# Low parts of v and of the softmax factors: identity products summed in PSUM in place of VectorE subtractions

## The chip, the cores and the metric

The kernel runs on one core of a Trainium2 chip. A core has five engines that run side by side, each through its own list of instructions: TensorE (PE, matrix products, results in PSUM), VectorE (DVE), ScalarE (ACT), GpSimd (POOL) and SyncE (SP, which here only starts transfers). They wait for each other by semaphores. The metric is the device time of one execution in microseconds; the lower the better.

## The reference

For each of 8 batches and 8 heads, with 576 positions, 64 values per head and 32 memory slots, all in fp32:

```python
a = softmax(phi)                                  # over the 32 slots
k_m = einsum('bhsm,bhsd->bhmd', a, k)
v_m = einsum('bhsm,bhsd->bhmd', a, v)
attn = softmax(q @ k_m.T / sqrt(64))
x = attn @ v_m                                    # heads side by side: (8, 576, 512)
scores = x @ w_gate
for b in range(8):                                # the 128 best positions of each batch
    h = relu(xe @ w1);  ye = h @ w2               # xe: the chosen rows; F = 1024
    out[b, top] = xe + sigmoid(score) * ye
```

The choice of the best 128 positions depends on small differences of the scores, so the kernel keeps close to fp32 all the way to the choice. That is why v and the softmax factors are split into two parts each before their product.

## The kernel before, in words

There are 16 groups, one for each batch and half of its heads (four heads). For each group the function `softmax` computes the softmax factors `e` in a [128, 576] tile (four heads x 32 slots by positions). It is long: 48 VectorE instructions per group with ScalarE instructions between them, since the exponential and its rounding are followed step by step. It ends with L276, and goes on to `keys`.

`keys` turns `e` on TensorE (L316, six 96-column blocks, two PSUM banks), copies it to SBUF with ScalarE (L318, tile `aS`), and then splits it: `hi` is `aS` with the lowest twelve mantissa bits cleared (L322, a bitwise and on VectorE), `lo` is `aS - hi` (L324, a subtraction on VectorE). GpSimd starts eight transfers that write `lo` and `hi` to the DRAM tensor `aparts` (L327). TensorE then multiplies `aS` with k (L333), and ScalarE stores the result in `kbd` (L338).

`split_v` does the same with v: a [128, 1152] tile per group is loaded (L285), `hi` by a bitwise and (L293), the low part by a subtraction in place (L295), and GpSimd starts the writes of both to `vparts` (L298). The next tile is loaded into one of two buffers.

`values` reads `vparts` and `aparts` back in another layout and sums the products of the parts over the positions (L371, 9216 small products in four stages of two batches). Attention (`centre`, `scores`, `attend`, `rank`, `gather`) and the expert layer (`ffn`, L625, L636, L646) follow for each batch.

The order of the work is written out by hand: every function is a generator, and a `yield` gives way. One pass of the main loop is called a turn here. In each turn, one call goes to the softmax (two chains of groups alternate at first: one has groups 0, 2, 4, 6 and then 8 to 15, the other 1, 3, 5, 7), one call in every second turn to `split_v`, then 7 calls (10 with attention, 12 once the softmax is done) to the sums, one to the attention and two to the expert layer. Attention starts when the short chain is done. The instructions enter each engine's list in this order, and a later instruction doesn't overtake an earlier one's place in its engine's list. A group takes 11 calls here, a v tile three.

The kernel has eight banks of PSUM: four hold the sums of `values`, and the other four go round as `bank` for all else until the sums are done.

Of the kernel before, what the change touches and what calls it, by code (L numbers as in the profile page):

```python
# [8 lines left out]
F32 = mybir.dt.float32  # L9
# [5 lines left out]
AF = mybir.ActivationFunctionType  # L15
# [4 lines left out]
P = 128  # L20
NC = 6
# [16 lines left out]
def kernel(  # L38
# [15 lines left out]
    nc = tc.nc  # L54
    ctx.enter_context(tc.manual_schedule())
    B, S, D = out.shape
# [6 lines left out]
    Dh = D // H  # L63
# [5 lines left out]
    scale = 1.0 / Dh ** 0.5  # L69
# [7 lines left out]
    const = ctx.enter_context(tc.tile_pool(name="const", bufs=1))  # L77
    weights = ctx.enter_context(tc.tile_pool(name="weights", bufs=1))
    rows = ctx.enter_context(tc.tile_pool(name="rows", bufs=1))
# [7 lines left out]
    vio = first.enter_context(tc.tile_pool(name="vio", bufs=2))  # L87
    more = []

    def bank(shape, dtype=F32, pool=None):  # L90
        pool = pool or (more or [pss])[0]
        return pool.tile(list(shape), dtype, tag="bank", name="bank")
# [11 lines left out]
    def load_q(b, j):  # L104
        qs[b, j] = step.tile([P, NPR, S // 2], F32, name="qb")
        nc.sync.dma_start(out=qs[b, j], in_=qT[b, :, :, j * (S // 2):(j + 1) * (S // 2)])

    groups = [(b, g) for b in range(B) for g in range(NG)]
# [4 lines left out]

    ident = const.tile([P, P], F32, name="ident")
    make_identity(nc, ident)

    kbd = [const.tile([P, NPR, 2 * M], F32, name=f"kbd{i}") for i in range(B)]
    vbd = [const.tile([P, 2, 4 * Dh], F32, name=f"vbd{i}") for i in range(3)]
# [63 lines left out]
    def softmax(i, ch):  # L182
# [3 lines left out]
        def t(name, dtype=F32):  # L186

            return ex.tile([P, NC * P if name in WIDE else S], dtype, name=name)[:, :S]
# [56 lines left out]
        dl, p = t("lo"), t("big")  # L245
# [29 lines left out]
            stt(out=e, in0=a0, scalar=sm[:, part:part + 1], in1=e, op0=ALU.mult, op1=ALU.add)  # L275
        stt(out=e, in0=e, scalar=sm[:, 1:2], in1=a0, op0=ALU.mult, op1=ALU.add)  # L276
        soft[i] = e
        yield
        yield from keys(i, ch)

    def split_v():

        def load(b, g):
            vb = vio.tile([P, 4 * S * Dh // P], F32, name="vb")
            nc.sync.dma_start(out=vb, in_=v[b, g])  # L285
            return vb

        coming = load(*groups[0])
        for i, (b, g) in enumerate(groups):
            vb = coming  # L290
            yield
            hi = vio.tile([P, 4 * S * Dh // P], F32, name="vhi")
            nc.vector.tensor_single_scalar(hi.bitcast(I32), vb.bitcast(I32), -4096,  # L293
                                           op=ALU.bitwise_and)
            nc.vector.tensor_sub(vb, vb, hi)  # L295
            yield
            for vp, src in enumerate((vb, hi)):
                nc.gpsimd.dma_start(  # L298
                    out=vparts[b, g, :, vp].rearrange("w r s d -> w (r s d)")
                                           .rearrange("w (p x) -> p w x", p=P),  # L300
                    in_=src.unsqueeze(1).to_broadcast([P, 2, 4 * S * Dh // P]))
            if i + 1 < len(groups):
                coming = load(*groups[i + 1])
            yield

    v_m = {}

    def keys(i, ch):
        ex, (b, g) = exs[ch], groups[i]
        a = soft.pop(i)  # L310
        kb = ks.pop(i)
        aS = ex.tile([P, NC * P], F32, name="lo")[:PT].rearrange("p (c m) -> p c m", m=P)
        for c0 in range(0, NC, 3):
            tp = bank([PT, 3, P])
            for c in range(3):
                nc.tensor.transpose(out=tp[:, c], in_=a[:, (c0 + c) * PT:(c0 + c + 1) * PT],  # L316
                                    identity=ident)
            nc.scalar.activation(aS[:, c0:c0 + 3], tp, AF.Copy)  # L318
        yield
        hi = ex.tile([P, NC * P], F32, name="big")[:PT].rearrange("p (c m) -> p c m", m=P)  # L320
        lo = ex.tile([P, NC * P], F32, name="low")[:PT].rearrange("p (c m) -> p c m", m=P)
        nc.vector.tensor_single_scalar(hi.bitcast(I32), aS.bitcast(I32), -4096,  # L322
                                       op=ALU.bitwise_and)
        nc.vector.tensor_sub(lo, aS, hi)  # L324
        for part, src in enumerate((lo, hi)):
            for h in range(4):
                nc.gpsimd.dma_start(  # L327
                    out=aparts[h, b, g, part].rearrange("(c p) m -> p c m", p=PT),
                    in_=src[:, :, h * M:(h + 1) * M])
        km = bank([P, 2, 2 * M])  # L330
        for rr in range(2):
            for c in range(NC):
                nc.tensor.matmul(out=km[:, rr], lhsT=kb[:, c, rr * P:(rr + 1) * P],  # L333
                                 rhs=aS[:, c, rr * 2 * M:(rr + 1) * 2 * M],
                                 start=(c == 0), stop=(c == NC - 1))
        for u in range(2):
            part = slice(u * Dh, (u + 1) * Dh)
            nc.scalar.activation(kbd[b][part, 2 * g:2 * g + 2, u * M:(u + 1) * M],  # L338
                                 km[part, :, u * M:(u + 1) * M], AF.Copy)
# [345 lines left out]
    def finish(job):  # L685
        for _ in job:
            pass
# [3 lines left out]
    def group(i, ch):  # L691
        at = order[ch].index(i)
        if at + 1 < len(order[ch]):
            load_phi(order[ch][at + 1], ch)
        yield from softmax(i, ch)
        made.append(i)

    def softmaxes():

        todo, live, since = [list(o) for o in order], {}, 6  # L700
        while any(todo) or live:
            for ch in range(2):
                if ch not in live and todo[ch] and since >= 6:
                    live[ch] = group(todo[ch].pop(0), ch)
                    since = 0
            since += 1
            for ch in list(live):
                if next(live[ch], live) is live:
                    del live[ch]
                yield  # L710

    def steps():

        return 12 if not working else 10 if attend_all else 7
# [13 lines left out]
    def attentions():  # L728

        todo, live, since = list(range(B)), [], 12  # L730
        while todo or live:
            if todo and todo[0] in summed and len(live) < 2 and since >= (12 if working else 8):
                live.append(attention(todo.pop(0)))
                since = 0
            since += 1
            for job in list(live):
                if next(job, live) is live:
                    live.remove(job)
            yield

    late_consts()
    w1_sb = weights.tile([P, KD, F], F32, name="w1_sb")
    w2_sb = weights.tile([P, KF, D], F32, name="w2_sb")
    working = [softmaxes(), split_v()]
    parts, sums, attend_all, products = None, all_sums(), None, ffns()
    turn = 0
    while True:
        turn += 1
        if turn == 8:
            nc.scalar.activation(ident16, ident, AF.Copy)  # L750
            nc.sync.dma_start(out=w1_sb, in_=w1.rearrange("(t p) f -> p t f", p=P))
            nc.sync.dma_start(out=w2_sb, in_=w2.rearrange("(t p) f -> p t f", p=P))
        if working and next(working[0], working) is working:
            working.pop(0)
        if len(working) == 2 and turn % 2:
            next(working[1], None)
        for _ in range(steps()):
            next(sums, None)
        if attend_all is None and set(order[1]) <= set(made):

            finish(working.pop(1))
            first.close()
            work, step, one = (
                ctx.enter_context(tc.tile_pool(name=name, bufs=2 - (name == "one"),
                                               reuse_waits="tile"))
                for name in ("step", "work", "one"))
            for j in range(2):
                load_q(0, j)
            eTs = [one.tile([P, 2, NT * P], F32, name=f"eT{i}") for i in range(2)]
            for t in eTs:  # L770
                nc.gpsimd.memset(t[:, :, S:], 0.0)
            attend_all = attentions()
        if attend_all and next(attend_all, working) is working:
            break
        for _ in range(2):
            next(products)
# [3 lines left out]
    ps = bank([1, B * NT])  # L780
# [46 lines left out]
```

## Time and profile before

The median of three runs is 1050.5 us (1049.24 to 1057.09). The profiled execution has a span of 1051.3 us.

| Engine | busy, us | share of the span |
|---|---|---|
| VectorE | 784.4 | 75% |
| TensorE products | 598.7 | 57% |
| TensorE weight loads (overlap the products) | 439.8 | 42% |
| ScalarE | 293.6 | 28% |
| GpSimd | 224.3 | 21% |

| Queue | MB | share of 16 DMA engines |
|---|---|---|
| started by SyncE | 94.14 | 29.5% |
| started by GpSimd | 70.27 | 19.7% |

A busy share is an average over the whole span. The rows of instructions give a line, the engine, what it writes and reads with its shape, how often, then the busy time and the mean of one in ns, then how long the engine was idle just before and what ended that. A row of waits gives who waited, for whom, the sum in us, how many times and the longest. An fp32 product shows as two records where the operands are plain fp32.

### The profile page before, as it was taken

Reading aid. Unit: us, or ns where it says so; the run is one execution under the profiler, and the core shown is the slowest. Engines: PE = TensorE matmul, PEld = TensorE weight load, DVE = VectorE, ACT = ScalarE, POOL = GpSimd, SP = SyncE. Lnnn points to the kernel's source line nnn. Section 1 sums busy time; section 2 is a strip of 40 time slices with the busy share of each in tenths; the row PEclk is TensorE's granted clock in tenths of the full one; section 3 lists DMA queues with packets and bytes.
Section 4 is the critical chain, followed back from the end, with each engine's and each line's share of the span. In section 5 each row is a group of like instructions: output and inputs, shape, how many; then the busy total and the mean of one; then the engine's idle time right before and its main releaser. Section 6 shows DMA issues by size and latency. Waiting matters only on the chain. (4 is left out here: it accounts for less than half of the span.)

```text
span 1051.3 us, 25384 instructions
## 1 busy us (share of the span) xinstructions
PE 598.7 (57%) x10738; PEld 439.8 (42%) x10738; DVE 784.4 (75%) x1342; ACT 293.6 (28%) x578; POOL 224.3 (21%) x335
## 2 busy tenths in 40 slices
PE   0021022255554355675567397875738969889795
PEld 0021022154443354554434374664415657544542
DVE  7899999899899968698786968698993336324940
ACT  2233233233233232323224342141432101213230
POOL 7030221220230230404113021402503011011110
PEclk9999999995665656877678699566866986989688
DMA  9364544677887825554613256463404466522320
GB/s 291 126 232 153 188 157 169 192 230 277 264 274 253 313 46 155 152 179 145 214 51 106 72 141 206 127 194 115 114 0 116 153 218 189 163 66 66 120 70 23
DMA packets 60714, 166.11 MB, mean 158 GB/s; under 512 B 10801, under 2 KB 21041, under 8 KB 60593
## 3 DMA queue, kind: packets, MB, share of 16 engines
q1 hardware_dynamic: 39088, 94.14, 29.5%
q0 software_dynamic: 21504, 70.27, 19.7%
q8 instruction: 87, 1.43, 0.6%
q14 instruction: 35, 0.28, 0.1%
HBM read 96.21 MB, written 68.16 MB: 156 GB/s over the span
## 5 line engine op out<-in xcount | busy, mean ns | idle before, releaser
L371 PE MATMUL acc<-a_rows,v_rows 32*64 32x128 f32 x9216 | 217.8, 257 | 106.7 <-DMA a_rows<-aparts 97.6
L371 PEld LDWEIGHTS acc<-a_rows,v_rows 32*64 32x64 f32 x9216 | 197.7, 167 | 150.2 <-issue 113.9
L316 PE MATMUL bank<-ident,e 128*96 128x128 f32 x96 | 22.5, 403 | 214.8 <-DVE e L276 204.6
L316 PEld LDWEIGHTS bank<-ident,e 128*96 128x96 f32 x96 | 16.0, 185 | 219.7 <-issue 183.4
L333 PE MATMUL bank<-lo,kb 96*128 96x64 f32 x384 | 67.0, 353 | 7.6 <-ACT lo L318 6.8
L333 PEld LDWEIGHTS bank<-lo,kb 96*128 96x128 f32 x384 | 65.5, 267 | 12.1 <-ACT lo L318 8.6
L327 POOL DMA_DIRECT2D aparts<-low x64 | 47.2, 746 | 104.5 <-DVE low L324 100.8
L646 PE MATMUL bank<-w_sb,hT 128*128 128x512 f32 x128 | 67.2, 661 | 0.0
L636 PE MATMUL bank<-w_sb,xeT 128*128 128x512 f32 x128 | 65.5, 647 | 2.9 <-ACT xeT L627 2.9
L530 PE MATMUL bank<-vbd,eT 128*128 128x256 f32 x160 | 60.0, 510 | 0.0
L221 DVE TENSOR_TENSOR lo<-lo,rh 128x576 f32<-128x576 f32 x64 | 56.7, 885 | 2.2
L176 ACT ACTIVATE vh<-num 128x576 int16<-128x576 f32 x32 | 21.8, 683 | 127.3 <-DVE num L225 116.7
L534 DVE TENSOR_TENSOR xj<-bank,rd 128x512 f32<-128x512 f32 x40 | 27.5, 688 | 36.8 <-PE bank L530 34.9
L537 POOL TENSOR_TENSOR xj<-xj,mean 128x1024 f32<-128x1024 f32 (+1 forms) x12 | 26.1, 2174 | 128.5 <-DVE xj L534 89.8
L583 DVE SCALAR_TENSOR_TENSOR cmp<-row,tg,wide 128x576 bf16<-128x576 f32 x40 | 32.5, 811 | 25.9 <-ACT row L569 25.1
L298 POOL DMA_DIRECT2D vparts<-vb x16 | 11.6, 726 | 186.2 <-DVE vb L295 161.9
L224 DVE TENSOR_TENSOR low<-low,lo 128x576 f32<-128x576 f32 x64 | 48.5, 758 | 2.2
L327 POOL DMA_DIRECT2D aparts<-big x64 | 46.7, 738 | 0.0
L220 DVE SCALAR_TENSOR_TENSOR lo<-num,vh 128x576 f32<-128x576 f32 x48 | 36.0, 751 | 13.2 <-ACT vh L176 13.2
L530 PEld LDWEIGHTS bank<-vbd,eT 128*128 128x128 f32 x160 | 35.0, 243 | 23.8 <-issue 19.6
L602 PE MATMUL bank<-tg,pick 128*128 128x2 f32 (+1 forms) x80 | 16.9, 329 | 47.4 <-DVE pick L597 20.2
L176 ACT ACTIVATE low<-big,c 128x576 f32<-128x576 f32 x16 | 12.4, 775 | 96.4 <-DVE big L247 96.4
(150 smaller groups left out, 1244.2 us busy)
## 6 DMA issues: line engine op xcount, KB each, us to landing
v_rows<-vparts SPq DMA_DIRECT2D x128, 288.0 KB
vparts<-vb POOLq DMA_DIRECT2D x16, 1152.0 KB, 5.2
vparts<-vhi POOLq DMA_DIRECT2D x16, 1152.0 KB, 8.9
a_rows<-aparts SPq DMA_DIRECT2D x512, 36.0 KB
vb<-in_v SPq DMA_DIRECT2D x16, 576.0 KB
kb<-in_k SPq DMA_DIRECT2D x16, 576.0 KB
qb<-in_qT SPq DMA_DIRECT2D x16, 576.0 KB
out<-xj POOLq DMA_DIRECT2D x16, 512.0 KB, 3.8
```

The costliest lines, as they stand in the source:

```text
L176: nc.scalar.activation(dst, src, func, bias=biases[c] if c else 0.0, scale=s)
L220: stt(out=lo, in0=val, scalar=GRID, in1=h, op0=ALU.mult, op1=ALU.subtract)
L221: tt(out=lo, in0=lo, in1=rh, op=ALU.mult)
L224: tt(out=low, in0=low, in1=lo, op=ALU.add)
L316: nc.tensor.transpose(out=tp[:, c], in_=a[:, (c0 + c) * PT:(c0 + c + 1) * PT], identity=ident)
L327: nc.gpsimd.dma_start(out=aparts[h, b, g, part].rearrange("(c p) m -> p c m", p=PT), in_=src[:, :, h * M:(h + 1) * M])
L333: nc.tensor.matmul(out=km[:, rr], lhsT=kb[:, c, rr * P:(rr + 1) * P], rhs=aS[:, c, rr * 2 * M:(rr + 1) * 2 * M], start=(c == 0), stop=(c = ...
L371: nc.tensor.matmul(out=accs[i][:Dh, :P].rearrange("p (h m) -> p h m", m=M), lhsT=vr[p, s], rhs=ar[p, :, s], start=(ch == 0 and s == 0), st ...
L530: nc.tensor.matmul(out=o[:, g * 4 * Dh:(g + 1) * 4 * Dh], lhsT=eT[:, g, (c0 + c) * P:(c0 + c + 1) * P], rhs=vbd[b % 3][:, g], start=False, ...
L583: nc.vector.scalar_tensor_tensor(out=cmp, in0=row, scalar=g, in1=wide[:, off:off + S], op0=ALU.is_equal, op1=ALU.mult, accum_out=equal[:, ...
L636: nc.tensor.matmul(out=ps[:n], lhsT=xeT[:, d, :n], rhs=w1_sb[:, d, f0:f0 + 512], start=(d == 0), stop=(d == KD - 1))
L646: nc.tensor.matmul(out=ps[:n], lhsT=hT[:, f, :n], rhs=w2_sb[:, f], start=(f == 0), stop=(f == KF - 1))
```

## The change

The subtractions leave VectorE. A new function `difference` makes x - y as two products that add up in one PSUM bank: the identity times x, and then the negated identity times y. ScalarE copies the bank to the place of the result, one `yield` later. The low part of v is made in three pieces of 384 columns, that of the softmax factors in two pieces of 384. The masks that make the high parts stay on VectorE. A constant `less_ident` is added. The `yield` after the end of the softmax goes away, and `split_v` is called in every turn, not in every second one. The purpose is to take work off VectorE and give it to TensorE and ScalarE.

```diff
     make_identity(nc, ident)
+    less_ident = const.tile([P, P], F32, name="less_ident")
+    nc.scalar.activation(less_ident, ident, AF.Copy, scale=-1.0)
...
         soft[i] = e
-        yield
         yield from keys(i, ch)
...
             vb = coming
             yield
-            hi = vio.tile([P, 4 * S * Dh // P], F32, name="vhi")
+            hi = vio.tile([P, n], F32, name="vhi")
             nc.vector.tensor_single_scalar(hi.bitcast(I32), vb.bitcast(I32), -4096,
                                            op=ALU.bitwise_and)
-            nc.vector.tensor_sub(vb, vb, hi)
-            yield
+            for x0 in range(0, n, n // 3):
+                x = slice(x0, x0 + n // 3)
+                yield from difference(vb[:, x], hi[:, x], vb[:, x])
             for vp, src in enumerate((vb, hi)):
                 nc.gpsimd.dma_start(
...
+    def difference(x, y, dst):
+
+        rows, n = x.shape
+        ps = bank([rows, n])
+        nc.tensor.matmul(out=ps, lhsT=ident[:rows, :rows], rhs=x, start=True, stop=False)
+        nc.tensor.matmul(out=ps, lhsT=less_ident[:rows, :rows], rhs=y, start=False, stop=True)
+        yield
+        nc.scalar.activation(dst, ps, AF.Copy)
...
         nc.vector.tensor_single_scalar(hi.bitcast(I32), aS.bitcast(I32), -4096,
                                        op=ALU.bitwise_and)
-        nc.vector.tensor_sub(lo, aS, hi)
+        for c0 in range(0, NC, 3):
+            yield from difference(*(x[:, c0:c0 + 3].rearrange("p c m -> p (c m)")
+                                    for x in (aS, hi, lo)))
         for part, src in enumerate((lo, hi)):
...
-        if len(working) == 2 and turn % 2:
+        if len(working) == 2:
             next(working[1], None)
```

More of the change, by code (lines that the diff above doesn't have):

```diff
@@ L286, in load @@
             return vb
-        coming = load(*groups[0])
+        coming, n = load(*groups[0]), 4 * S * Dh // P
         for i, (b, g) in enumerate(groups):
@@ L300, in split_v @@
                                            .rearrange("w (p x) -> p w x", p=P),
[L301 removed]
+                    in_=src.unsqueeze(1).to_broadcast([P, 2, n]))
             if i + 1 < len(groups):
```

## The prediction

> **What bounds the kernel now.** I read the totals and the slices first, then the same sums over three stretches, because the totals average over stages with different limits. The stretches are cut where the eighth and the sixteenth softmax group end (337.0 and 789.7 us are the starts of the instruction that ends them, L276; the last of their key products follows some 10 us later).
>
> ```profile
> PE 598.7 (57%) x10738; PEld 439.8 (42%) x10738; DVE 784.4 (75%) x1342; ACT 293.6 (28%) x578; POOL 224.3 (21%) x335
> ...
> PE   0021022255554355675567397875738969889795
> ...
> DVE  7899999899899968698786968698993336324940
> ```
>
> ```profile
> 15.00:345.00 330.00, 103.46 (x2362) 95.32 (x2363) 302.04 (x457) 100.02 (x160) 65.82 (x101) 0.87 0.64 218
> 345.00:802.00 457.00, 289.99 (x5530) 218.16 (x5529) 369.62 (x657) 140.26 (x291) 115.19 (x148) 0.72 0.45 135
> 802.00:1051.30 249.30, 205.24 (x2849) 126.30 (x2848) 101.71 (x226) 51.83 (x126) 28.93 (x52) 0.86 0.37 117
> ```
>
> The columns after the length are the busy times of PE, PE's weight loads, DVE, ACT and POOL, then granted clock, DMA share and GB/s. Stage one (two softmax chains and the splitting of v) is VectorE: 302 of 330 us, 92%. Stage two (one chain, with attention) is VectorE at 81% with PE at 63%. Stage three has no softmax; PE is busy 82% of it, VectorE 41%.
>
> The chain of work that ended last reaches back only to 939 us and is mostly the expert layer's products (L646, L636), so it says nothing about the changed lines. The waits say more:
>
> ```profile
> PE bank L316 <- DVE e L276: 204.6, 12, 58.4
> DVE rd L522 <- PE bank L517: 25.2, 8, 5.5
> DVE big L322 <- ACT lo L318: 6.0, 5, 2.2
> SPq L285 <- DMA vparts<-vb: 153.9, 8, 28.2
> ```
>
> PE waits for VectorE at 12 of 16 groups, so up to there PE is ahead. VectorE's waits for PE and ScalarE are short and lie in the attention; between 200 and 300 us, say, all its listed waits come to 5.6 us. The last line: the load of the next v tile starts when the write of an older one has landed.
>
> **What the Trainium skill says.** "VectorE: DVE Perf Modes", the section on the 1x mode, gives one fp32 result per cycle for an operation on two tensors, at 0.96 GHz: 1152 elements are 1.20 us, and the trace has 1.36 for the subtraction of v (L295). The one-tensor mask (L293) takes 0.77 for the same size. So the subtraction is the dear half of the split. "TensorE: Matmul & The Clock Gate", Part 1, says that PE runs at half rate after an idle window of about 3.4 us and at full rate after a busy one. The trace agrees in its durations: four records of one shape (L646) take 3.62 us at 756 us and 1.98 at 766 us; its clock column, which shows 1.00 for the nearly idle first 200 us, does not show this. The same page ("Architectural detail") calls ScalarE's and VectorE's queues strictly first in, first out. In the trace no ScalarE copy overtakes one that waits for PE (L338 waited 48.8 us in 14 times). That is the danger here: a copy out of PSUM that waits holds the softmax's own ScalarE work.
>
> **The change part by part.**
>
> ```profile
> L295 DVE TENSOR_TENSOR vb<-vb,vhi 128x1152 f32<-128x1152 f32 x16 | 21.7, 1358 | 0.6
> L324 DVE TENSOR_TENSOR low<-lo,big 96x768 f32<-96x768 f32 x16 | 15.3, 954 | 0.5
> L293 DVE TENSOR_SCALAR vhi<-vb 128x1152 int32<-128x1152 int32 x16 | 12.2, 765 | 0.0
> L318 ACT ACTIVATE lo<-bank 96x384 f32<-96x384 f32 x32 | 14.5, 484 | 25.7 <-PE bank L316 25.6
> ```
>
> Removed: 16 subtractions of 1.358 us for v (21.7 us, all before 348 us) and 16 of 0.954 us for the softmax factors (15.3 us, half in each of the first two stages). Stage one loses 21.7 + 7.6 = 29.3 us of VectorE, stage two 7.6.
>
> Added on PE: 48 pairs of products for v (three thirds of 16 tiles) and 32 for the factors, each 384 columns wide in fp32. A pair leaves four records, since one fp32 product leaves two (64 products with w2 are 128 records of L646). The row with four records of 512 columns, scaled by 384/512, gives 1.98 x 0.75 = 1.5 us with PE busy, and 3.62 x 0.75 = 2.7 after idling. 80 pairs are 120 to 216 us. In stage one 64 pairs at 2.7 are 173 us on top of 103, which fits into 300; in stage two 16 pairs at 1.5 are 24 us on top of 290 of 457. As an average it hides behind VectorE.
>
> Added on ScalarE: 80 copies from PSUM of the shape of L318, 0.484 us each: 39 us, 31 of them in stage one, which goes from 100 to 131 us of about 310. It hides too, unless a copy waits for PE. The one-time negated identity costs a ScalarE instruction of some 0.3 us (the cast of the identity, L750, takes 292 ns) before the first softmax needs that engine: nothing.
>
> Moved: the copy comes one turn after its pair, so PE has a turn's time. A softmax group takes 12 calls instead of 11: two yields more in the key part, one fewer after e. A v tile takes 5 turns instead of 6 (five calls at every turn, three at every other before).
>
> New waits, stage one. A group took 40.4 us (e ends at 215.64 and 256.09 start to start). Without 0.95 us and 11/6 x 1.36 us of subtraction, with 2.4 masks per group where there were 1.83, it would be 37.4 us, or 3.1 us a turn. While the value sums run beside the v split (order of the instructions: after group 4, up to v tile 16, about 24 turns), PE has per turn: 56 sum products, 1.63 us (112 in 3.25 us at 218 us); key work 6.9/12 = 0.57; 0.6 v pairs and 0.17 key pairs, 1.15 to 2.1 us. That is 3.35 to 4.3 us against 3.1. The excess over 24 turns is 6 to 28 us. Behind a late pair stand, on PE, the sums and the transposes; on ScalarE, behind its copy, the next softmax instructions; and VectorE waits for those. I take 8, near the low end, because PE this full does not go idle for long.
>
> New waits, stage two. The transposes now stand in the same turn as e, so the mask (L322) comes one turn after e and not two:
>
> ```profile
> 215.64 0.82 DVE L276 SCALAR_TENSOR_TENSOR e<-e,sm,vh 128x576 f32<-128x576 f32 x1
> ...
> 216.61 1.49 PE L316 MATMUL bank<-ident,e 128*96 128x128 f32 x6 [11.90 <-DVE e L276]
> ...
> 218.77 0.87 ACT L318 ACTIVATE lo<-bank 96x384 f32<-96x384 f32 x2
> ```
>
> From the end of e to the end of the copies are 3.2 us. In stage one the other chain fills it. In stage two a turn is 457/88 = 5.2 us, of which softmax work is some 3.2, so about 2 us of attention cover it and 1.2 us stay open at 8 groups: 9 us, less what was already waited, 7. Behind the mask stand all of VectorE's attention instructions. ScalarE, which holds its copies until the transposes are done, keeps back the exponentials queued behind them; I count that in the 7.
>
> Stage three. Eight more turns in stage two, at two product steps each, bring 16 wide products forward: 64 of 128 come before the last group's keys in program order, 48 before. At 0.88 us (16 records in 7.07 us) that is 14 us of PE out of the PE-bound tail; at 82% busy some 10 us come off. VectorE's instructions after the last group stay 194 against 199.
>
> Sum: 1050.5 - 29.3 + 8 - 7.6 + 7 - 10 = **1018.6 us**.
>
> **The rivals.** *PE and ScalarE become the coupling that sets the pace.* Stage one then gives back 28 of 29.3 us; in stage two the whole 3.2 us is exposed at each of 8 groups (26 us against the 7.6 saved), and the 38 us of PE work added there (24 and 14) cost VectorE another 11, in the ratio of its present idling. With 10 off the tail: 1050.5 - 1.3 + 18 + 11 - 10 = 1068, slower. For it speak PE's 63% in stage two and the waits of L522 and L534 on PE; against it the 204.6 us that PE waits for e.
>
> *The v loop becomes too short.* A v tile used to come every 22 us, now every 15.5. From its mask: three turns to the last copy (9.3), issue 0.7, landing of the write 5.2 to 9.6, then the load of the tile after next, whose landing the trace does not show; I bound it by the writes' 4.7 below and 9.6 above. That makes 20 to 29 us of the 31 that two periods give, and the load also stands behind the sums' loads in SyncE's queue, which waited 159.9 us for PE. With a wait of 1.5 us at 13 tiles 20 us are lost: 1038. Against it: L293 never waited before, and DMA share is 0.64 in stage one.
>
> *Everything hides.* 37 us of VectorE and 14 us of the tail come off, and the 8 us for which GpSimd waited at the stage change for the last write of v (L771) go too: 1050.5 - 37 - 14 - 8 = 991.
>
> **How the numbers follow.** Chances: the sum above 0.52, coupled 0.17, v loop 0.17, all hidden 0.14. Faster by over 1% (under 1040) are the first and the last and half of the v loop, with a little off for the first's upper edge: 0.73. Within 1%: 0.10, slower: 0.17. The range runs from just under the all-hidden case (988) past the v loop to 1058, which takes in the coupled case only where its waits come to about two thirds of what is assumed above.
>
> **What would show it.** Right: VectorE's busy time near 747 us; the eighth group's e ending near 315 to 320 us, not 338; the copies on ScalarE with short waits for PE (a few us in all per stage); the mask L294 without waits for the load of v; 16 more wide products before the last group; the tail about 240 us. Wrong: VectorE waiting for ScalarE in stage one by more than 15 us in all, ScalarE's copies waiting for PE by tens of us, PE at 9 tenths between 180 and 300 us, or the mask of the factors waiting over 2 us per group. The forecast fails most easily on the shared order: if a late PE stops ScalarE and so VectorE, the 37 us removed are waited out instead.

## The result and the profile after

The changed kernel takes 1124.0 us (median of four runs, 1122.14 to 1131.9) against 1049.9 us: a ratio of 1.071, interval 1.063 to 1.079. It is 7% slower, where 3% faster was forecast. Ratios here leave out executions that are over 1.5% above the fastest of their kernel, so that a ratio can differ a little from that of two medians; the profiled executions of e5 and e8 were such ones and are not read.

The page of the kernel after, totals and the slices of PE and VectorE (tenths of busy time; a slice is 28 us):

```profile
PE 721.9 (64%) x11058; PEld 483.5 (43%) x11058; DVE 746.9 (67%) x1310; ACT 327.6 (29%) x659; POOL 225.6 (20%) x335
...
PE   2256546666555374973846668678674878888795
...
DVE  8898998863578949397596765958758445303950
```

VectorE has lost the 37 us that were meant (784.4 to 746.9) and is no longer full: in the ninth to eleventh slices (224 to 308 us), where it had eights and nines before, it has a six, a three and a five. PE is not full there either, with five and six tenths. Neither is the bound there; the engines wait for each other.

The same by stage. The cuts are 203 us (the fifth group has ended and the value sums begin), the end of the eighth group and of the sixteenth. Columns as in the table of before:

```profile
15.00:203.00 188.00, 93.77 (x288) 54.63 (x289) 169.31 (x267) 75.41 (x136) 43.73 (x69) 0.74 0.67 228
203.00:357.00 154.00, 92.83 (x2185) 67.60 (x2183) 99.48 (x159) 44.47 (x80) 24.55 (x34) 0.75 0.63 201
357.00:865.00 508.00, 326.59 (x5734) 227.16 (x5734) 364.29 (x653) 154.55 (x317) 108.24 (x138) 0.74 0.40 115
865.00:1120.50 255.50, 207.12 (x2850) 133.56 (x2850) 102.95 (x231) 51.37 (x126) 34.71 (x60) 0.82 0.38 117
```

Subtracting the fourth column from the second gives VectorE's idle time. Stage one (the first two rows): 73 us, where it was 28; stage two: 144 against 87; stage three: 153 against 148. That is 106 us of new idling less 37 us of removed work: the 69 us by which the span grew. The first row is as forecast: 169 of 188 us, 90%; from the first to the fifth group there are 37.3 us to each (e starts at 53.99 and at 203.36). All of stage one's loss lies in the second row, where VectorE is at 65%.

What VectorE waits for, and in the last line PE, in the waits of the kernel after (who, for whom, us in all, times, longest):

```profile
DVE xj L547 <- PE bank L543: 54.9, 22, 6.2
DVE lo L222 <- ACT vh L178: 29.9, 18, 11.1
DVE vhi L294 <- DMA vb<-in_v: 28.3, 2, 17.8
...
DVE big L333 <- ACT lo L329: 17.8, 13, 3.1
...
PE bank L327 <- DVE e L278: 100.6, 14, 18.2
```

The second and third lines are stage one: the softmax waits for a ScalarE rounding (L178), and the mask of v waits for its load. PE's wait for the softmax, which had spoken for "PE is ahead", fell from 204.6 to 100.6 us.

The greater part of the loss lies in stage two: from the start of the eighth e to that of the sixteenth it takes 507.6 us, where it took 452.7, and VectorE's listed waits went from 67 to 132 us. The largest of them, from 357 to 865 us:

```profile
DVE xj L547 <- PE bank L543: 33.0, 11, 6.2
DVE at L628 <- ACT gr L623: 17.0, 4, 5.3
DVE less L602 <- ACT sign L594: 17.0, 3, 8.3
DVE big L333 <- ACT lo L329: 13.3, 7, 3.1
DVE eT L474 <- ACT th L472: 10.7, 2, 10.2
```

In the kernel before, from 345 to 802 us, these were 15.5, 2.0, none, 6.0 and 0.5 us. The fourth is the mask of the factors; the others lie in the attention, which the change doesn't touch.

One stall of stage one, in the order of time of the kernel after. First PE (start, duration, what, and in brackets the idle time before and what ended it):

```profile
218.49 0.48 PE L384 MATMUL acc<-a_rows,v_rows 32*64 32x128 f32 x8 [5.28 <-DMA a_rows<-aparts]
218.90 1.59 PE L312 MATMUL bank<-lo,ident 96*96 96x384 f32 x2
220.29 1.49 PE L313 MATMUL bank<-big,less_ident 96*96 96x384 f32 x2
221.57 1.49 PE L312 MATMUL bank<-vb,ident 128*128 128x384 f32 x2
222.85 1.32 PE L313 MATMUL bank<-vhi,less_ident 128*128 128x384 f32 x2
```

Then ScalarE and VectorE:

```profile
216.38 0.76 ACT L178 ACTIVATE rl<-den,c 128x576 f32<-128x576 f32 x1
224.20 0.49 ACT L315 ACTIVATE vb<-bank 128x384 f32<-128x384 f32 x1 [7.06 <-PE bank L313]
224.59 0.48 ACT L315 ACTIVATE low<-bank 96x384 f32<-96x384 f32 x1
230.50 0.45 ACT L351 ACTIVATE kbd<-bank 64x64 f32<-64x64 f32 x2 [5.43 <-PE bank L346]
230.98 0.49 ACT L315 ACTIVATE vb<-bank 128x384 f32<-128x384 f32 x1
231.37 0.68 ACT L178 ACTIVATE vh<-num 128x576 int16<-128x576 f32 x1
```

```profile
220.22 0.76 DVE L227 SCALAR_TENSOR_TENSOR num<-big,low 128x576 f32<-128x576 f32 x1
232.07 0.76 DVE L222 SCALAR_TENSOR_TENSOR lo<-num,vh 128x576 f32<-128x576 f32 x1 [11.09 <-ACT vh L178]
```

Read it from the end. VectorE idles 11.1 us for `vh`, a rounding whose input was ready at 221. ScalarE reaches it at 231, since copies stand ahead of it in its list (L315, L351), and two of them wait for PE, 7.1 and 5.4 us. PE is late because it stood 5.3 us before a sum product whose `a_rows` had not been loaded; behind that stand the identity products and the key products. A transfer is late, and the whole row of engines stands.

Such a wait of PE is not new. First the kernel before from 203 to 345 us, then the kernel after from 203 to 357 us:

```profile
PE acc L371 <- DMA a_rows<-aparts: 35.3, 15, 7.1
PE bank L316 <- DVE e L276: 31.6, 4, 11.9
```

```profile
PE acc L384 <- DMA a_rows<-aparts: 26.3, 11, 6.7
PE bank L327 <- DVE e L278: 9.1, 2, 8.8
```

The kernel before waits longer for these loads, but no wait of its VectorE there is over 0.8 us. What went is PE's time in hand: its wait for e falls from 31.6 to 9.1 us. In stage two the waits for `a_rows` didn't grow either (27.7 us, 30.7 before).

### The profile page after: what moved, and what is told of

The parts are those of the page before. It is cut to its first block, busy times and chain, and to the rows that moved or that the text cites. A ratio compares the mean times of both kernels' runs of the same rounds, so it can differ in the third digit from the quotient of the medians.

```text
span 1120.5 us, 26125 instructions
## 1 busy us (share of the span) xinstructions
PE 721.9 (64%) x11058; PEld 483.5 (43%) x11058; DVE 746.9 (67%) x1310; ACT 327.6 (29%) x659; POOL 225.6 (20%) x335
## 3 DMA queue, kind: packets, MB, share of 16 engines
q1 hardware_dynamic: 39088, 94.14, 28.3%
## 5 line engine op out<-in xcount | busy, mean ns | idle before, releaser
L384 PE MATMUL acc<-a_rows,v_rows 32*64 32x128 f32 x9216 | 206.3, 247 | 79.0 <-DMA a_rows<-aparts 76.2
L384 PEld LDWEIGHTS acc<-a_rows,v_rows 32*64 32x64 f32 x9216 | 185.3, 156 | 136.1 <-issue 80.1
L313 PE MATMUL bank<-vhi,less_ident 128*128 128x384 f32 x96 | 52.7, 639 | 72.0 <-DVE vhi L294 66.2
L327 PE MATMUL bank<-ident,e 128*96 128x128 f32 x96 | 21.2, 384 | 100.6 <-DVE e L278 100.6
L649 PE MATMUL bank<-w_sb,xeT 128*128 128x512 f32 x128 | 72.7, 709 | 8.7 <-ACT xeT L640 4.8
L312 PE MATMUL bank<-vb,ident 128*128 128x384 f32 x96 | 53.6, 649 | 34.2 <-DMA vb<-in_v 33.8
L313 PEld LDWEIGHTS bank<-vhi,less_ident 128*128 128x128 f32 x96 | 23.5, 256 | 95.0 <-DVE vhi L294 73.0
L222 DVE SCALAR_TENSOR_TENSOR lo<-num,vh 128x576 f32<-128x576 f32 x48 | 38.3, 797 | 30.2 <-ACT vh L178 29.9
L178 ACT ACTIVATE vh<-num 128x576 int16<-128x576 f32 x32 | 21.8, 682 | 110.4 <-DVE num L227 96.4
L346 PEld LDWEIGHTS bank<-lo,kb 96*128 96x128 f32 x384 | 51.5, 216 | 4.6 <-issue 2.0
L346 PE MATMUL bank<-lo,kb 96*128 96x64 f32 x384 | 52.5, 301 | 0.6 <-ACT vb L315 0.6
L223 DVE TENSOR_TENSOR lo<-lo,rh 128x576 f32<-128x576 f32 x64 | 50.5, 789 | 2.2
```

The source lines that it names most:

```text
L222: stt(out=lo, in0=val, scalar=GRID, in1=h, op0=ALU.mult, op1=ALU.subtract)
L223: tt(out=lo, in0=lo, in1=rh, op=ALU.mult)
L312: nc.tensor.matmul(out=ps, lhsT=ident[:rows, :rows], rhs=x, start=True, stop=False)
L313: nc.tensor.matmul(out=ps, lhsT=less_ident[:rows, :rows], rhs=y, start=False, stop=True)
L384: nc.tensor.matmul(out=accs[i][:Dh, :P].rearrange("p (h m) -> p h m", m=M), lhsT=vr[p, s], rhs=ar[p, :, s], start=(ch == 0 and s == 0), st ...
L649: nc.tensor.matmul(out=ps[:n], lhsT=xeT[:, d, :n], rhs=w1_sb[:, d, f0:f0 + 512], start=(d == 0), stop=(d == KD - 1))
```

## The experiments

e1 to e18 are variants of the two kernels. The text quoted below the code of each is what was expected of it before it ran. Code cuts are marked by dots.

### The order alone, and the two halves

e1 keeps the order of the changed kernel, each yield and each call, and has VectorE subtract again, in the same three and two pieces.

```diff
     def difference(x, y, dst):
-        ps = bank([rows, n])
-        nc.tensor.matmul(out=ps, lhsT=ident[:rows, :rows], rhs=x, start=True, stop=False)
-        nc.tensor.matmul(out=ps, lhsT=less_ident[:rows, :rows], rhs=y, start=False, stop=True)
+        nc.vector.tensor_sub(dst, x, y)
         yield
-        nc.scalar.activation(dst, ps, AF.Copy)
```

> The changed order of calls is kept (12 calls per softmax group, a v tile in five calls at every turn, no yield after e), but the low parts are subtractions on VectorE again, in the places where the identity products stood. First theory (the new products and copies couple the engines): VectorE carries its 37 us again and nothing waits for PE, so 1045 to 1060 us, stage two (end of the 8th to end of the 16th softmax group) about 455 us as before. Rival (the order of calls itself is what costs): stage two stays near 500 us and the whole at 1095 to 1125 us.

Measured 1118.6 us, ratio 1.064 (1.059 to 1.069). The order costs about 66 us without one identity product (4 us of them are VectorE's own work, which grows from 784.4 to 788.7 us with the smaller pieces). From here to the changed kernel are 5 us, within the two intervals: the products and copies don't earn the 37 us of VectorE. The five waits of stage two listed above stand in e1 as well (26.9, 12.6, 12.5, 13.3 and 9.5 us), so most of them comes with the order and not with the products.

e2 makes v's low parts as changed and leaves the factors as before, with the yield after e. e3 is the other half: the factors as changed, without that yield, and v as before.

```diff
 e2, against the changed kernel:
         soft[i] = e
+        yield
         yield from keys(i, ch)
...
-        for c0 in range(0, NC, 3):
-            yield from difference(...)
+        nc.vector.tensor_sub(lo, aS, hi)
 e3, against the changed kernel:
-            for x0 in range(0, n, n // 3):
-                ...
+            nc.vector.tensor_sub(vb, vb, hi)
+            yield
...
-        if len(working) == 2:
+        if len(working) == 2 and turn % 2:
```

> Only v is split by identity products, called in every turn; the softmax factors are subtracted on VectorE and the yield after e is back (11 calls per group). First theory (coupling): stage one about 357 us as in the changed kernel against 338 before, since all three long stalls there lie between v products, the sums and the loads of v; stage two 455 us; 1065 to 1080 us in all. Rival (order of calls): stage one as in the changed kernel, stage two 453 us, so this run does not tell them apart, but it gives the share of v: if it is under 1050 us, v is not at fault at all.

> Only the softmax factors are split by identity products, with 12 calls per group and no yield after e; v is subtracted on VectorE at every second turn as before. First theory (coupling): stage one is about 7 us shorter than before (330), stage two about 505 us, 1090 to 1105 us in all. Rival (order of calls): the same stage two. If stage two is near 455 us, the loss there in the changed kernel was handed on from stage one and is not the key part's own.

e2: 1062.8 us, 1.009 (1.0045 to 1.0126). e3: 1115.5 us, 1.0625 (1.0575 to 1.0675). Nearly all of the loss comes with the factors, which have the smaller part of the work: 7.6 us of VectorE in each of two stages. e3 also has the 12th call and lacks the yield, where e2 has 11 calls and the yield.

### The yield after e

e4 puts that one `yield` back into the changed kernel; e5 takes it out of the kernel before.

```diff
 e4, against the changed kernel:
         soft[i] = e
+        yield
         yield from keys(i, ch)
 e5, against the kernel before:
-        yield
         yield from keys(i, ch)
```

> The changed kernel with the yield after e put back (13 calls per group), so that transposes and their copies come one turn after e. If the copies of the transposes, which hold ScalarE until e is done, are what costs in stage two: its length falls from 508 to about 480 us and the whole to 1095 to 1105 us. If the longer group (more attention calls per softmax group) is what costs: stage two grows to 520 us or more, the whole is 1125 to 1140 us.

> The kernel before with nothing changed but the yield after e taken out (10 calls per group, transposes and their copies in the same turn as e). Theory A (transposes in the turn of e put PE and ScalarE behind e, and the attention of that turn behind them): stage two some 20 us longer, 1065 to 1080 us. Theory B (what costs is only the number of calls in which the softmax gives VectorE little or nothing): one such call fewer, so 1030 to 1050 us.

e4: 1096.4 us, 1.044 (1.038 to 1.050), 28 us less than the changed kernel, 23 of them in stage two. e5: 1081.3 us, 1.026 (1.016 to 1.036), about 2.6% for a yield alone. The two agree: some 28 us. Without the yield the transposes and the copies of `lo` stand in the same turn as e, and hold ScalarE and then the mask (L333: 17.8 us of waits, 6.0 before). That is less than half of the 28 us; in stage two of e4 the waits for `sign` are gone too and those for `gr` are 6.7 us. e4 gives the yield, a 13th call, back and is faster, so a long group is not in itself the cost of this part.

### More calls per group

e6 leaves the kernel before as it is, subtractions and all, and gives a group two calls with nothing in them. e12 is e6 with fewer calls of the sums per turn, so that a group of 13 calls has about as many calls of the sums beside it as one of 11 did: 78 where it was 77 in stage one, 104 for 110 in stage two. e13 does the same to the changed kernel, with 77 and 110.

```diff
 e6, against the kernel before:
         nc.vector.tensor_sub(lo, aS, hi)
+        for _ in range(2):
+            yield
 e12, against e6:
-        return 12 if not working else 10 if attend_all else 7
+        return 12 if not working else 8 if attend_all else 6
 e13, against the changed kernel:
-        return 12 if not working else 10 if attend_all else 7
+        if not working:
+            return 12
+        per_group = 110 if attend_all else 77
+        return turn * per_group // 12 - (turn - 1) * per_group // 12
```

> The kernel before with two more yields in the key part, between the subtraction and the transfers (13 calls per group, the yield after e kept, all subtractions on VectorE). Theory B: two calls without softmax work more per group, VectorE idles in them for PE's share of the turn, some 4 us in 8 groups: stage two 480 to 490 us as with the yield put back, 1080 to 1100 us. Theory A alone: the same time as before, 1045 to 1060 us.

> The run with two thin calls more per group (all subtractions on VectorE), but with 6 and 8 calls of the sums per turn where there were 7 and 10, so that a group again sees 78 and 104 of them (77 and 110 before, 91 and 130 with the thin calls alone). Theory C (more calls per group mean more sums per group, whose loads come one part in 3.1 us at best, so PE falls behind, holds ScalarE's copies and so VectorE): the loss of 40 us goes, 1050 to 1065 us, stage one near 337 us. Theory B (VectorE idles in the thin calls whatever the sums do): 1080 to 1095 us.

> The changed kernel with nothing altered but the sums per turn, so that a group of 12 calls again sees 77 calls of the sums in stage one and 110 in stage two (84 and 120 in the changed kernel). Theory C (more sums per group is what costs): one more call per group carries about half of what two carried (29 us), so 15 to 30 us come off: 1090 to 1108 us. If the products themselves make PE late: 1115 us or more.

e6: 1092.9 us, 1.042 (1.034 to 1.050). Two empty calls cost about 40 us. e12: 1063.9 us, 1.011 (1.004 to 1.019): with fewer sum steps per turn, about 29 of the 40 go. e13: 1088.2 us, 1.034 (1.026 to 1.041), 36 us off the changed kernel, in both stages: the eighth group's e starts at 337.6 us instead of 356.8, and the stretch from there to the sixteenth takes 486.0 instead of 507.6.

This shows that fewer sum steps per turn help once calls have been added. It doesn't show that the sum steps of the added calls are the loss. Before the start of the eighth e the traces have 2016 sum products in the kernel before, in the changed kernel and in e1, and from there to the sixteenth 4896 in all three, since the sums of two batches begin only when their four groups are done. The added call puts more sums beside a group while they run, but not into the stage. In e6 there are 2232 before the eighth e, in e12 1920 and in e13 1824, fewer than in the kernel before. That kernel with fewer sum steps and nothing else changed was not run.

A stall of e6 has no identity product in it. PE, ScalarE, VectorE:

```profile
286.51 1.33 PE L373 MATMUL acc<-a_rows,v_rows 32*64 32x128 f32 x40 [4.97 <-DMA a_rows<-aparts]
287.78 5.38 PE L335 MATMUL bank<-lo,kb 96*128 96x64 f32 x24
```

```profile
280.27 0.76 ACT L176 ACTIVATE rl<-den,c 128x576 f32<-128x576 f32 x1
293.20 0.45 ACT L340 ACTIVATE kbd<-bank 64x64 f32<-64x64 f32 x2 [12.16 <-PE bank L335]
293.67 0.68 ACT L176 ACTIVATE vh<-num 128x576 int16<-128x576 f32 x1
```

```profile
294.38 0.76 DVE L220 SCALAR_TENSOR_TENSOR lo<-num,vh 128x576 f32<-128x576 f32 x1 [9.51 <-ACT vh L176]
```

PE waits for a load of the sums, its key products come late, ScalarE stands 12.2 us before their copy with the rounding of the softmax behind it, and VectorE stands 9.5 us. It is the stall of the changed kernel in a kernel that has only two more yields.

Why the load is late: SyncE's list in the kernel after (start, the time of the issue, line):

```profile
300.71 0.50 SPq L363 DMA_DIRECT2D v_rows<-vparts  x1
301.26 2.45 SPq L370 DMA_DIRECT2D a_rows<-aparts  x4
303.80 0.50 SPq L363 DMA_DIRECT2D v_rows<-vparts  x1
```

One chunk of the sums is five issues, 3.09 us here with nothing to hold them (300.71 to 303.80), and a chunk is nine calls. While the sums run in stage one, a group of 12 calls has 84 sum steps beside it, 9.3 chunks and 28.8 us of SyncE; one of 11 had 77, 8.6 chunks and 26.4 us. At the forecast 37.4 us per group SyncE would be 77% taken by these issues, where it was 65% of 40.4 (estimates from these figures). That the loads are late because of this is inferred and not shown. A rival stands: SyncE itself waits for PE to give back the buffers of the sums, 42.9 us in ten times between 203 and 357 us, and 26.8 in eight between 203 and 345 us before. No run separates the two.

### The load of v

The third of VectorE's waits above is `vhi` for the load of v, 28.3 us in two. e8 is e2 with a third buffer and each load issued two tiles ahead; e11 does that to the changed kernel.

```diff
-            vb = vio.tile([P, 4 * S * Dh // P], F32, name="vb")
+            vb = vio.tile([P, 4 * S * Dh // P], F32, name="vb", bufs=3)
...
-        coming, n = load(*groups[0]), 4 * S * Dh // P
+        coming, n = [load(*groups[0]), load(*groups[1])], 4 * S * Dh // P
...
-            vb = coming
+            vb = coming.pop(0)
...
-            if i + 1 < len(groups):
-                coming = load(*groups[i + 1])
+            if i + 2 < len(groups):
+                coming.append(load(*groups[i + 2]))
```

> Only v by identity products at every turn, as in the run with v alone, but with three buffers for the v tiles and their loads started two tiles ahead. If stage one's loss there is the late load of v (12.6 us waited by the mask and what follows from it): the stalls go and VectorE's 21.7 us come out, stage one 315 to 322 us, 1030 to 1040 us in all. If it is PE that holds ScalarE's copies behind the sums: the mask's wait goes but the time stays at 1055 to 1065 us.

> The changed kernel with three buffers for v and loads two tiles ahead. If the late load of v makes the stalls of 10.5 and 17.8 us: stage one 325 to 332 instead of 357 us, stage two as in the changed kernel (505 us), 1090 to 1100 us. If the stalls come from PE, late by the sums: stage one stays over 345 us.

e8: 1051.9 us, 0.993 (0.990 to 0.996), against 1.009 for e2: with the load ahead, v's low parts from TensorE lose nothing. A gain isn't shown, since the kernel before beside it has a median of 1052.5 us; the time fits neither expectation. e11: 1110.9 us, 1.0545 (1.047 to 1.062), 13 us off the changed kernel, and `vhi` waits 0.2 us instead of 28.3. Its eighth e starts at 345.8 us, just past the 345 of the second case. The gain is under half of that wait, since other waits grew in its place: `lo` for `vh` (L222) in stage one has 37.1 us, from 26.7.

### The products themselves

e7 keeps the 11 calls and the yield, and makes only the factors' low parts by products, with the copies in the same call as their products.

```diff
 against the changed kernel, with the yield and v as before:
-            yield from difference(*(x[:, c0:c0 + 3].rearrange("p c m -> p (c m)")
-                                    for x in (aS, hi, lo)))
+            finish(difference(*(x[:, c0:c0 + 3].rearrange("p c m -> p (c m)")
+                                for x in (aS, hi, lo))))
```

> Only the softmax factors by identity products, but with each copy in the same call as its pair, so that a group has 11 calls and the yield after e as before. Both theories (the order costs, not the products): stage two 445 to 465 us, 1040 to 1060 us. Rival (the products and copies cost by themselves, through copies that hold ScalarE for PE): 8 groups with 4 to 6 us more, 1080 us or more.

e7: 1093.9 us, 1.038 (1.030 to 1.046). Stage one takes 28 us more than before, its eighth e starting at 364.8. A copy that follows at once on its products makes ScalarE wait through them: 64.2 us in all at these copies, against 22.6 in e3, where a call lies between. Whether that is worth the call isn't shown, as e7 and e3 differ in the yield after e too.

e17 is the changed kernel with the products in bf16, on the upper 16 bits of each number (with a bf16 identity and its negative): it leaves the lower 16 bits out of the low parts, so they are not the reference's. The order and the copies stay.

```diff
-        nc.tensor.matmul(out=ps, lhsT=ident[:rows, :rows], rhs=x, start=True, stop=False)
-        nc.tensor.matmul(out=ps, lhsT=less_ident[:rows, :rows], rhs=y, start=False, stop=True)
+        nc.tensor.matmul(out=ps, lhsT=ident16[:rows, :rows], rhs=x.bitcast(BF16)[:, 1::2], start=True, stop=False)
+        nc.tensor.matmul(out=ps, lhsT=less16[:rows, :rows], rhs=y.bitcast(BF16)[:, 1::2], start=False, stop=True)
```

> The changed kernel with the same short bf16 products (low parts wrong, order and copies unchanged). Order alone was 66 us with the subtractions on VectorE; with 37 us of them gone and PE unburdened, 1085 to 1100 us if PE's time is what the products cost; 1115 or more if it is not.

e17: 1100.4 us, 1.052 (1.047 to 1.057), 1.8% or some 20 us below the changed kernel. PE's busy time falls by 71 us (721.9 to 650.8). So a good quarter of that time had reached the end, and it was costed as hidden.

### Attempts at a version that keeps the gain

e9 folds the factors' low part into the first two calls of the chain's next group, so that a group keeps 11 calls, with v as in e8. e10 has the same for the factors and v as before. e15 is e9 with the high part written to DRAM at once and a tile of its own for the low part; e16 is e15 with the bf16 products of e17 (low parts wrong in the same way).

```diff
 e9, against the changed kernel with the yield back and v's loads ahead:
+    def low_part(i, aS, hi, lo):      # the products, copies and writes of keys
+        ...
+    def more_of(ch):
+        if ch in late:
+            next(late[ch], None)      # called in the next group's first two calls
...
-        for c0 in range(0, NC, 3):
-            yield from difference(...)
-        ...
+        late[ch] = low_part(i, aS, hi, lo)
+        next(late[ch])
 e15, against e9:
-        lo = ex.tile([P, NC * P], F32, name="low")...
+        lo = ex.tile([P, NC * P], F32, name="klo")...
...
+        write_part(b, g, 1, hi)
         late[ch] = low_part(i, aS, hi, lo)
```

> Both low parts by identity products, v with loads two tiles ahead, and the second half of the key part (copies, second pair, transfers) folded into the first two calls of the chain's next group, so that a group has 11 calls and the yield after e. If only the order of the calls is at fault, VectorE's 37 us come out in both stages: stage one 310 to 320, stage two 440 to 455 us, 1015 to 1035 us in all. If the products and copies cost by themselves: 1050 us or more.

> The same folding for the softmax factors alone; v as before. If only the order is at fault: 15.3 us less VectorE, stage one about 330, stage two 445 to 453 us, 1035 to 1045 us. If products and copies cost by themselves, as in the run with copies in the same call (1094 us): 1070 us or more.

> Folding of the key part into the next group's calls as before (11 calls, yield after e, v ahead), but the high part is written out at once as in the kernel before, and the low part has a tile of its own. The first folding made VectorE wait 77 us for the write of the high part, 12 times 6.5 us. Those 77 us go: 1060 to 1075 us if products and copies leave nothing over, less than 1050 if they hide as forecast.

> The folded kernel with own tile, its identity products taken on the upper 16 bits of both operands as bf16, so that the low parts come out wrong and each product is one short record in place of two. The order and the copies are the same. If PE's time for the products is what they cost: 1066 falls by 20 to 35 us, to 1030 to 1045. If it is the copies or the order: 1058 to 1068.

e9: 1148.6 us, 1.090 (1.082 to 1.098); e10: 1157.4 us, 1.097 (1.090 to 1.104). Both are slower than the changed kernel, for a reason that the waits of e10 name:

```profile
DVE big L226 <- DMA aparts<-big: 77.4, 12, 9.5
```

The next group's softmax rewrites the buffer of `hi`, whose write to DRAM had been put off with the low part. This is a flaw of the attempt and says nothing on the change. e15, without it: 1065.5 us, 1.013 (1.009 to 1.016). e16: 1054.9 us, 1.005 (1.002 to 1.008). In e15 all 37 us are gone from VectorE, the calls per group are those of before, the yield is there and the loads are ahead, and it is still slower than e8, which has the factors subtracted on VectorE, by 2% of the ratios (1.3% if the medians are compared). The waits of e15 show where ScalarE stands, first from 15 to 345 us and then from 345 to 800 us:

```profile
ACT kbd L370 <- PE bank L365: 36.5, 8, 7.6
```

```profile
ACT kbd L370 <- PE bank L365: 53.9, 8, 13.7
```

Before, these copies of the key products waited 48.8 us in the whole run, 6.1 of it in stage one. But in e2, with v alone by products, it is 27.2 us to 345 and 43.5 from there to 800 us, so only some 10 us in each stage can come with the factors. e16 gives back 0.8%, between its two forecasts: part of e15's loss is PE's time for the products. The rest may lie with the place of the copies; it was not split further.

e14 puts all three remedies into the changed kernel: the yield, the loads ahead, and the pace of the sums for 13 calls.

```diff
         soft[i] = e
+        yield
...
+        per_group = 110 if attend_all else 77
+        return turn * per_group // 13 - (turn - 1) * per_group // 13
 and v's loads as in e11
```

> The changed kernel with three things mended and the products kept: the yield after e back (13 calls), the sums spread so that a group sees 77 and 110, and v loaded two tiles ahead in three buffers. If order, pace and loads are the whole cause: 27 from the yield (measured), about 20 to 35 from the pace, 13 from the loads come off 1124, so 1045 to 1065 us. If the products cost by themselves: 1075 us or more.

e14: 1095.7 us, 1.040 (1.032 to 1.047). This missed: alone, the remedies had given 28, 36 and 13 us, together they give 28. That is what the yield alone gave (e4, 1096.4 us), so on top of it pace and loads gave nothing. Which waits they share was not traced. Against e12, which has the same 13 calls and nearly the same pace but subtracts on VectorE, e14 is 2.8% slower.

e18 takes the lesson of the pace to e8: six calls of the sums per turn in stage one instead of seven.

```diff
-        return 12 if not working else 10 if attend_all else 7
+        return 12 if not working else 10 if attend_all else 6
```

> v by identity products with loads two tiles ahead, as in the run of that name, but with 6 calls of the sums per turn in stage one where there were 7. If the sums' pace is what still holds stage one at 338 us (44 to 48 us per group after the fifth): it falls to 320 to 328 us and the whole to 1030 to 1040 us, unless the sums, finished later, hold the first attention. If not the pace: 1045 to 1055 us.

e18: 1043.0 us, 0.989 (0.978 to 0.999), far below the changed kernel and some 1% below the kernel before, with four executions and an interval that all but reaches 1. Against e8 the intervals overlap, so that a gain from the pace isn't shown; the time lies between its two forecasts. Stages one and two of e18:

```profile
15.00:339.00 324.00, 164.61 (x2231) 111.71 (x2229) 281.15 (x440) 117.69 (x206) 68.79 (x113) 0.70 0.66 221
339.00:780.00 441.00, 303.74 (x5851) 227.47 (x5850) 370.05 (x654) 142.41 (x296) 111.89 (x145) 0.74 0.47 137
```

VectorE idles 71 us in stage two, where it idled 87 before and 144 in the changed kernel; in stage one 43, for 28 and 73. The eighth e starts 6 us earlier than before (330.7, for a forecast of 320 to 328).

## Why the prediction was wrong, step by step

**The bound.** Right for before: VectorE at 92% in stage one, and the first five groups of the changed kernel took 37.3 us each, as the 37.4 of the sum. Part of that is luck: the sum starts from 40.4 us, but over the same groups the kernel before took 39.5, so 2.2 us came off and not 3.0. It holds only until the value sums begin.

**Removed and added.** Right. VectorE's busy time is 746.9 us for "near 747". A pair of products takes 1.49 us in a busy stretch (210.79 to 212.28) and 2.67 us after idling (218.90 to 221.57), forecast 1.5 and 2.7; the 80 pairs have 165 us in all, within 120 to 216. The copy takes 0.479 us for 0.484.

**"As an average it hides behind VectorE."** Failed in part: e17 shows some 20 us of PE's time for the products reaching the end. Their average fits, but PE's lateness in single turns passes to ScalarE's copies.

**"Moved" and the new waits.** This is the step that failed. The two terms for the waits of the new order were 8 us in stage one and 7 in stage two; VectorE's idle time grew by 45 and 56 us. The order alone, without a product, costs 66 us (e1). Three things were missed or priced too low:

1. A call has a price of its own. The prediction spread the same 37.4 us over 12 turns, so that the 12th call cost nothing. Two empty calls cost 40 us (e6). It set PE's sum products of a turn against the turn, but not the loads that they wait for, nor the copies behind them: fewer sum steps per turn take 29 us from the two empty calls (e12) and 36 us from the changed kernel (e13). How much of this is the added call's doing isn't shown, since the sums in each stage are as many as before.
2. The yield taken away after e: I left "1.2 us open at 8 groups", in all 7 us with what stood behind. e4 and e5 measure about 28.
3. The load of v. The rival of the v loop named it and gave it 20 us; the trace has 28.3 us of waits in two, and e11 gives 13 us back.

The three overlap (e14), so they must not be added.

**The tail.** It was to lose 10 us and lost 5.4 (256.2 us instead of 261.6, counted from the start of the last group's e). The 16 wide products did move: 64 come before the last group's key products, 48 before. e18 and e1, with tails of 273.1 and 257.9 us, suggest that a longer stage two and a shorter tail go together.

**The rivals.** The coupled rival had the sign (1068) and the chain (ScalarE held by PE, VectorE by ScalarE), but took PE for full. It isn't: 60% busy between 203 and 357 us. In the stalls shown PE is late, not full, since it has waited for a load. None of the rivals gave one more turn a price.

**The signs named beforehand.** VectorE's waits for ScalarE in stage one exceed the 15 us (26.7 in L222 alone), and ScalarE's copies wait for PE by tens of us (L315 24.8 for v, 26.8 for the factors): both "wrong" signs came true. PE at nine tenths did not, nor did 2 us per group at the mask of the factors (17.8 us in 16 groups).

**Open.** How the 66 us of the order divide, in stage two above all, where the loads of the sums are waited for no longer than before. Why the remedies are worth so little together. Whether fewer sum steps per turn would help the kernel before by themselves. And why the factors' low parts on TensorE lose 1 to 2% even with calls, yield and loads as they should be (e15 against e8), beyond the 0.8% of PE's time (e16 against e15).

## What to carry to other kernels

In a program whose order is written out in turns, an empty call is not free: here two of them per group cost 40 us. Count what a turn holds per unit of work before and after the change, down to the queue that issues its transfers, and then check the count in the trace: here more sums stood beside each group while they ran, but no more in the stage. An engine that is idle on average may still be late, and a copy from PSUM in the list of a shared engine passes its lateness on to all that stands behind: price the queue behind the copy, not the copy. Run the new order with the old operations first; here one such run put 66 us on the order and left 5 us, within the noise, to the products and copies with all that they save and cost.

## What the runs showed beyond that

The same 24 key product records took 5.38 us in e6 after PE had waited for a load, and 2.89 us in the changed kernel at 369 us, amid other products; a late PE thus becomes later still. The other way round, the key products are shorter where identity products stand between them: all 384 records took 52.5 us in the changed kernel and 60.3 in e17 with its short products, but 67.0 in the kernel before and 72.8 in e1. That the identity products keep PE from idling fits these times; no run tests it apart.

From e's eighth start to the sixteenth, e18 took 436.8 us where the kernel before took 452.7, though it had put sums off into that stretch (5256 sum products for 4896). Of these 16 us the tail takes 12 back (273.1 us for 261.6).
